# Stage one of three FFT batches: one float32 matmul a channel replaced by three float32r matmuls on split words

## The chip, the core and the metric

The kernel runs on one core of one Trainium2 chip. The metric is device time in microseconds (us), from the first to the last instruction plus what the device needs around them; lower is better. The engines that matter here are TensorE (PE, matmuls; PEld is its weight load), VectorE (DVE), ScalarE (ACT), GpSimd (POOL) and SyncE (SP, which here issues most DMAs). Each engine works through its own instructions in order; they meet at semaphores.

## The reference

The reference is a long convolution with a learned filter, followed by a two-layer MLP on every token:

```python
h_filt = (np.maximum(pos_emb @ w1, 0.0) @ w2) * np.exp(-0.01 * pos)[:, None]
u = x * v                                            # (4, 12480, 128)
Uf = np.fft.rfft(u, n=2 * S, axis=1)
Hf = np.fft.rfft(h_filt, n=2 * S, axis=0)
y = np.fft.irfft(Uf * Hf[None], n=2 * S, axis=1)[:, :S, :]
z = (x * y).reshape(49920, 128)
h = np.maximum(z @ w_in, 0.0)                        # 128 -> 2048
out = h * h @ w_out                                  # 2048 -> 128
```

There are four batches of 12,480 tokens with 128 channels. The convolution is done per batch, the MLP per token.

## The kernel before

The FFT is written as four matmul stages (`stage1` to `stage4`), with the time axis folded to 112 x 112 positions. `stage1` multiplies x by v, folds the two halves of each row (a sum and a difference, into a tile `ut` of 112 partitions x 4 channels x 120 columns), and multiplies each channel's 112 x 120 block with a table `ef` of 112 x 208. The filter and batch 0 run it in a first part of the program with `big=True`; that branch is not changed. Batches 1, 2 and 3 run `fft(b, done)`, in which `stage1(b, False)` is the first of four generators.

From about 320 us on, the program is one long loop over MLP chunks of 510 tokens. A *step* is one pass of its inner loop (L872 to L900): `m_h` makes six float32r matmuls into a PSUM tile `A` (two buffers), `m_o` makes six float32r matmuls for the step before last into `O`, ACT takes relu and square (`m_g`), DVE forms the product and the low word (`m_l`). Both operands of these matmuls are kept in two float32r words, high and low, and `mm3` (L97) adds the three products high-high, low-high and high-low. Between these the loop calls `adv(1)`, `adv(2)` and `adv(3)`, which move the FFT generator on to its next `yield`; a generator that stands at `yield 1` is moved by `adv(1)` alone. So the order on each engine is set by the code: at `adv(1)`, a stage 1 step issues the loads for three groups ahead, the products and folds (`mul`) for two groups ahead, and the eviction of the group before (`evac`); at `adv(3)` it issues `mm(t)`, the matmuls of one group of four channels. One step holds one group, and 32 groups make a batch. Before the first group, `mul(0)` and `mul(1)` are issued at the end of one step, and `mm(0)` comes at the end of the second step after that.

For these three batches `mul` runs on POOL (L278, L280, L281: product, sum, difference), `evac` on ACT (L316 to L318) and DVE (L309, L310). Pool `s1` has two buffers by default, three for `ut` (`halves`), three for `xt`, two for `vt`. A float32 matmul shows in the trace as two PE records; a float32r matmul as one. The rows name tiles by the program's names: `F` is one PSUM bank of stage results, `zi`, `zh` and `zl` are an MLP chunk's input and its two words (`zsplit`, once in eight steps), `gh` and `gl` the two words of the squared activations.

Of the kernel before, what the change touches and what calls it, by code (L numbers as in the profile page):

```python
# [7 lines left out]
F32 = mybir.dt.float32  # L8
F32R = mybir.dt.float32r
# [8 lines left out]
I = 112  # L18
C = 104
S = C * I  # L20
# [21 lines left out]
KP = 64 + HI  # L42
# [7 lines left out]
def hyena_moe_kernel(  # L50
# [19 lines left out]
    nc = tc.nc  # L70
# [14 lines left out]
    def pool(name, side="left", **kw):  # L85
        return tc.tile_pool(name=name, bufs=kw.pop("bufs", 2), side=side, reuse_waits="tile", **kw)

    def bank():
        return psf.tile([128, 512], F32, tag="F", name="F")
# [6 lines left out]

    def mm3(o, L, R, first=True, last=True):  # L97
        lh, ll = L
        rh, rl = R
        nc.tensor.matmul(o, lh, rh, start=first, stop=False)  # L100
        nc.tensor.matmul(o, ll, rh, start=False, stop=False)  # L101
        nc.tensor.matmul(o, lh, rl, start=False, stop=last)  # L102
# [48 lines left out]
    def first_rows():  # L151
        return W[:I].rearrange("p t (q d) -> p (t q) d", q=4)[:, : I + 1]
# [78 lines left out]
    def rest(k):  # L231
        for _ in range(k):
            yield 1
            yield 2
            yield 3

    def stage1(b, big, side="left", hook=None):
        DC = 4
        n = D // DC
        filt = b is None  # L240
        gap = HI + 1 if filt else HI
        with pool("s1", side) as p:
            ef = p.tile([I, 2, 2 * C] if big else [I, 2 * C], F32, name="ef", bufs=1)
            nc.sync.dma_start(out=ef, in_=e_tab[:, 2:4] if filt else e_tab[:, 0:2] if big else e_tab[:, 0])
            if not big:
                sign = p.tile([KP, 2], F32, name="sign", bufs=1)
                nc.gpsimd.memset(sign[:, 0:1], 1.0)
                nc.gpsimd.memset(sign[:, 1:2], -1.0)
            per = 2 if big else 1
            pa = 1  # L250
            L = {}
            halves = [p.tile([I, DC, KP], F32, name=f"ut{k}", bufs=1) for k in range(3)]
            for ut in halves:
                nc.gpsimd.memset(ut[:, :, gap:64], 0.0)

            def load(t):
                if filt or t >= n or t % per:
                    return
                xt = p.tile([128, per * DC, I], F32, tag="xt", name="xt", bufs=3)
                vt = p.tile([128, per * DC, I], F32, tag="vt", name="vt", bufs=3 if big else 2)  # L260
                queue = nc.gpsimd if big and t < early else nc.sync
                queue.dma_start(out=xt, in_=xs[b, :, t * DC : (t + per) * DC, :])
                queue.dma_start(out=vt, in_=vs[b, :, t * DC : (t + per) * DC, :])
                for k in range(per):
                    L[t + k] = [x[:I, k * DC : (k + 1) * DC] for x in (xt, vt)]

            def mul(t):
                if t >= n:
                    return
                ut = halves[t % 3]  # L270
                if filt:
                    f = first_rows()[:, :, t * DC : (t + 1) * DC].rearrange("p j d -> p d j")
                    eng = nc.vector
                    eng.tensor_add(out=ut[:, :, :gap], in0=f[:, :, HI:], in1=f[:, :, HI::-1])
                    eng.tensor_sub(out=ut[:, :, 64:], in0=f[:, :, HI + 1 :], in1=f[:, :, HI - 1 :: -1])
                else:
                    xt, vt = L[t]
                    (nc.vector if big else nc.gpsimd).tensor_mul(out=xt, in0=xt, in1=vt)  # L278
                    eng = nc.vector if big else nc.gpsimd
                    eng.tensor_add(out=ut[:, :, :HI], in0=xt[:, :, :HI], in1=xt[:, :, HI:])  # L280
                    eng.tensor_sub(out=ut[:, :, 64:], in0=xt[:, :, :HI], in1=xt[:, :, HI:])  # L281
                L[t] = ut

            def mm(t):
                u = L.pop(t)
                paired = big and t < n - 1
                if paired:
                    both = psa.tile([128, 2, 512], F32, tag="A", name="A")
                A = []
                for h in range(DC // 2):  # L290
                    A.append(both[:, h, :] if paired else bank())
                    for k in range(2):
                        o = A[h][:KP, k * 2 * C : (k + 1) * 2 * C]
                        if big:
                            nc.tensor.matmul(o[:64], u[:, 2 * h + k, :64], ef[:, 0, :], start=True, stop=True)
                            nc.tensor.matmul(o[64:], u[:, 2 * h + k, 64:], ef[:, 1, :], start=True, stop=True)  # L296
                        else:
                            nc.tensor.matmul(o, u[:, 2 * h + k, :], ef, start=True, stop=True)  # L298
                return A

            def evac(t, A):
                for h in range(DC // 2):
                    d0 = t * DC + 2 * h
                    view = W.rearrange("p t (k r d) -> p (t k) r d", k=2, r=2)[:, :C, :, d0 : d0 + 2]
                    src = A[h][:KP, : 4 * C].rearrange("p (d c r) -> p c r d", d=2, r=2)
                    if big:
                        (nc.vector.tensor_copy if h and t == n - 1 else nc.scalar.copy)(view, src)
                    elif h:
                        nc.vector.tensor_copy(view[:64], src[:64])  # L309
                        nc.vector.tensor_mul(  # L310
                            out=view[64:],
                            in0=src[64:, :, ::-1],
                            in1=sign[64:].rearrange("p (c r d) -> p c r d", c=1, d=1).to_broadcast([HI, C, 2, 2]),
                        )
                    else:
                        nc.scalar.copy(view[:64], src[:64])  # L316
                        nc.scalar.copy(view[64:, :, 0], src[64:, :, 1])
                        nc.scalar.mul(view[64:, :, 1], src[64:, :, 0], -1.0)  # L318

            la = 6 if big else 3  # L320
            early = 6 if big else 2
            for t in range(early):
                load(t)
                if big:
                    yield 1
            if not big:
                yield from rest(2)
            for t in range(pa + 1):
                mul(t)
            for t in range(early, la):  # L330
                load(t)
            yield 1
            yield 2
            prev = None
            for t in range(n):
                yield 1
                load(t + la)
                mul(t + pa + 1)
                if prev is not None:
                    evac(t - 1, prev)  # L340
                yield 2
                yield 3
                prev = mm(t)
                if hook is not None:
                    hook(t - n)
            yield 1
            evac(n - 1, prev)
# [332 lines left out]
    def fft(b, done):  # L680
        for name, gen in ("s1", stage1(b, False)), ("s2", stage2(False, False)), ("s3", stage3(False)), ("s4", stage4(b, done)):
            for k in gen:
                stage[0] = name
                yield k
# [41 lines left out]
    def during_s2(t):  # L726
# [3 lines left out]
        if t % TC == 0 and TH <= t // TC + 3 < NP // TC:  # L730
            table(t2s, t // TC + 3, tabs[0])

    s1f = stage1(None, True, "left")
    idle(10)
    filter_mlp(tables)
# [6 lines left out]
    raws = load_weights(wp)  # L742
    run(s1f)
    s1 = stage1(0, True, "right", during_s1)
    cvp = take("cvp")
    conv = [convert_weights(cvp, wp, raws, wt, range(k, 2 * NCW, 2)) for k in range(2)]
# [125 lines left out]
    for i in range(NM):  # L872
        for f in range(NS):
# [8 lines left out]
            while len(late) > len(tail):  # L882
                x, y, st = late.pop(0)
# [8 lines left out]
            n = i * NS + f  # L892
# [152 lines left out]
```

## Time and profile before

| | |
|---|---|
| median of 3 runs | 3071.08 us (3069.71 to 3072.46) |
| the profiled execution | 3062.8 us |
| its span, first to last instruction | 3060.9 us |
| PE busy | 3021.9 us, 99% of the span |
| DVE, ACT, POOL busy | 82%, 78%, 48% |
| stage 1 matmuls of batches 1 to 3 | 768 records, between 487.8 and 2009.1 us |

The page has the busy time of each engine, a picture of the span in 40 slices and the costliest groups. Matmul ends are modelled and overlap the next start, so the time that a stream of matmuls needs is read from start to start in the timeline, not from durations. The idle time in square brackets is what the engine waited before that instruction, and for whom.

### The profile page before, as it was taken

To read this page: it belongs to the slowest core of one execution; us is meant where nothing else is said; L and a number is where in the kernel's file an instruction comes from. 1 tells how busy PE (TensorE), PEld (TensorE's weight loads), DVE (VectorE), ACT (ScalarE), POOL (GpSimd) and SP (SyncE) were. 2 spreads that over 40 slices of the span, in tenths; PEclk is the share of its full clock that TensorE was granted. 3 is DMA by queue.
4 is the path that set the end of the run, shared out by engine and by line. 5 is a ranking of instruction groups with operands and counts; after the bars stand their busy time and mean duration, and the time that the engine had idled before them with its cause. 6 is when DMAs were issued, how large, how long until landed. Compare 5 with 4: busy or idle time off the path is not lost.

```text
span 3060.9 us, 48765 instructions
## 1 busy us (share of the span) xinstructions
PE 3021.9 (99%) x16010; PEld 2557.2 (84%) x16010; DVE 2510.9 (82%) x3056; ACT 2389.7 (78%) x3110; POOL 1469.1 (48%) x1595
## 2 busy tenths in 40 slices
PE   9989999999999999999999999999999999999999
PEld 8768888878888888888888888888888888888887
DVE  7888888878878988878877898878877898777776
ACT  5557777777888787788888877788888877888887
POOL 1249665647544665556544665646544563000000
PEclk9999999999999999999999999999999999999999
DMA  5782665444101664334200575434300474000000
GB/s 181 275 291 75 158 170 139 120 116 148 44 22 47 166 169 124 117 109 125 80 15 27 139 179 145 131 93 120 104 22 15 111 177 109 25 24 26 24 26 20
DMA packets 288753, 322.00 MB, mean 105 GB/s; under 512 B 95716, under 2 KB 214484, under 8 KB 288500
## 3 DMA queue, kind: packets, MB, share of 16 engines
q1 hardware_dynamic: 259348, 268.40, 30.3%
q0 software_dynamic: 29152, 50.48, 6.3%
q8 instruction: 128, 2.10, 0.3%
q14 instruction: 125, 1.02, 0.1%
HBM read 230.35 MB, written 64.55 MB: 96 GB/s over the span
## 4 chain that ended last, share of the span: by engine, by line
PE 88%; DMA 3%; DVE 3%; POOL 2%; issue 2%; ACT 1%; SPq 1%; DVEq 0%; ACTq 0%; POOLq 0%
PE A L100 11%; PE A L101 11%; PE A L102 11%; PE O L102 8%; PE O L101 8%; PE O L100 8%; PE F L386 5%; PE F L498 5%; PE F L298 4%; PE F L100 4%; PE F L102 4%; PE F L101 4%; PE A L296 2%; POOL W L411 1%; DMA xt<-x 1%
## 5 line engine op out<-in xcount | busy, mean ns | idle before, releaser
L800 ACT ACTIVATE r<-A 128x1020 f32<-128x1020 f32 (+2 forms) x784 | 804.2, 1026 | 410.7 <-PE A L102 397.1
L819 DVE TENSOR_TENSOR gl<-r,gh 128x1020 fp32r<-128x1020 f32 (+1 forms) x434 | 637.3, 1468 | 105.1 <-ACT r L807 68.1
L100 PE MATMUL A<-zh,wt 128*128 128x510 f32 (+2 forms) x1568 | 667.3, 426 | 1.8 <-DVE gl L819 1.5
L101 PE MATMUL A<-zh,wt 128*128 128x510 f32 (+2 forms) x1568 | 610.2, 389 | 0.0
L102 PE MATMUL A<-zl,wt 128*128 128x510 f32 (+2 forms) x1568 | 609.9, 389 | 0.0
L803 ACT ACTIVATE gh<-r 128x1020 fp32r<-128x1020 f32 (+1 forms) x452 | 477.3, 1056 | 61.0 <-PE O L101 53.3
L102 PE MATMUL O<-gl,wt 128*128 128x510 f32 (+1 forms) x1216 | 475.8, 391 | 3.6 <-DVE gl L819 3.5
L805 DVE SCALAR_TENSOR_TENSOR A<-A,r 128x1020 f32<-128x1020 f32 (+1 forms) x349 | 424.3, 1216 | 64.9 <-ACT r L800 63.0
L819 DVE TENSOR_TENSOR gl<-A,gh 128x1020 fp32r<-128x1020 f32 (+1 forms) x349 | 425.2, 1218 | 63.5 <-ACT gh L803 20.3
L101 PE MATMUL O<-gh,wt 128*128 128x510 f32 (+1 forms) x1216 | 472.1, 388 | 0.0
L100 PE MATMUL O<-gh,wt 128*128 128x510 f32 (+1 forms) x1216 | 472.0, 388 | 0.0
L807 ACT ACTIVATE r<-r 128x1020 f32<-128x1020 f32 (+1 forms) x435 | 461.0, 1060 | 12.5
L814 DVE CAST gh<-r 128x1020 fp32r<-128x1020 f32 (+1 forms) x332 | 232.6, 701 | 211.7 <-ACT r L807 210.7
L783 POOL TENSOR_TENSOR zl<-zi,zh 128x510 fp32r<-128x510 f32 (+1 forms) x97 | 126.6, 1305 | 536.1 <-PE A L102 427.7
L571 POOL TENSOR_TENSOR al<-W,ah 104x512 fp32r<-104x512 f32 x214 | 282.2, 1319 | 187.8 <-ACT ah L565 185.8
L102 PEld LDWEIGHTS A<-zl,wt 128*128 128x128 f32 x1568 | 294.4, 188 | 63.1
L507 POOL TENSOR_TENSOR W<-c 104x224 f32<-104x224 f32 x256 | 215.5, 854 | 264.6 <-ACT c L505 261.5
L100 PEld LDWEIGHTS A<-zh,wt 128*128 128x128 f32 x1568 | 296.0, 189 | 51.2 <-DVE gl L819 4.7
L101 PEld LDWEIGHTS A<-zh,wt 128*128 128x128 f32 x1568 | 296.3, 189 | 42.7
L423 POOL TENSOR_TENSOR W<-W,m 112x256 f32<-112x256 f32 x156 | 167.9, 1076 | 229.0 <-DVE m L421 207.0
L102 PEld LDWEIGHTS O<-gl,wt 128*128 128x128 f32 x1216 | 228.0, 187 | 53.0 <-DVE gl L819 5.7
L101 PEld LDWEIGHTS O<-gh,wt 128*128 128x128 f32 x1216 | 227.8, 187 | 47.5
(126 smaller groups left out, 5413.2 us busy)
## 6 DMA issues: line engine op xcount, KB each, us to landing
ht<-Hd SPq DMA_DIRECT2D x208, 256.0 KB
tb<-t POOLq DMA_DIRECT2D x224, 208.0 KB, 3.5
xt<-x SPq DMA_DIRECT2D x224, 128.0 KB
xt<-xs SPq DMA_DIRECT2D x96, 224.0 KB
vt<-vs SPq DMA_DIRECT2D x96, 224.0 KB
zd<-zs SPq DMA_DIRECT2D x333, 64.0 KB
out<-ot SPq DMA_DIRECT2D x79, 255.0 KB
tb<-t2s SPq DMA_DIRECT2D x156, 112.0 KB
```

The lines of the kernel that those rows point to most:

```text
L100: nc.tensor.matmul(o, lh, rh, start=first, stop=False)
L101: nc.tensor.matmul(o, ll, rh, start=False, stop=False)
L102: nc.tensor.matmul(o, lh, rl, start=False, stop=last)
L423: nc.gpsimd.tensor_sub(out=re[0], in0=re[0], in1=im[1])
L507: nc.gpsimd.tensor_sub(out=dst[:, 1], in0=c[:, :, 0:3:2], in1=c[:, :, 3:0:-2])
L571: eng.tensor_sub(out=lo, in0=w, in1=hi.bitcast(F32))
L800: nc.scalar.activation(r, h, AF.Relu)
L803: nc.scalar.activation(hi, r, AF.Square)
L805: nc.vector.scalar_tensor_tensor(out=h, in0=h, scalar=0.0, in1=r, op0=ALU.max, op1=ALU.mult)
L807: nc.scalar.activation(r, r, AF.Square)
L814: nc.vector.tensor_copy(hi, g)
L819: nc.vector.tensor_sub(out=lo, in0=g, in1=hi.bitcast(F32))
```

## The change

For the three batches the table `ef` and each group's folds `ut` are split into two float32r words, and each channel's one float32 matmul becomes the three float32r matmuls of `mm3`. The high word of `ut` is copied by ACT in even groups and by DVE in odd ones (480 values in each of 112 partitions); the low word is a subtraction on POOL. The split of a group is issued one step ahead of its matmuls, behind the `mul` for two groups ahead; `split(0)` is issued in the setup, behind `mul(1)`.

```diff
             if not big:
+                eh, el = (p.tile([I, 2 * C], F32R, name=f"e{k}", bufs=1) for k in range(2))
                 sign = p.tile([KP, 2], F32, name="sign", bufs=1)
...
-            L = {}
+            L, S = {}, {}
...
+            def split(t):
+                if big or t >= n:
+                    return
+                u = L[t]
+                hi, lo = (p.tile([I, DC, KP], F32R, tag=k, name=k) for k in ("uh", "ul"))
+                (nc.vector.tensor_copy if t % 2 else nc.scalar.copy)(hi, u)
+                nc.gpsimd.tensor_sub(out=lo, in0=u, in1=hi.bitcast(F32))
+                S[t] = hi, lo
+
             def mm(t):
                 u = L.pop(t)
+                words = S.pop(t, None)
...
-                            nc.tensor.matmul(o, u[:, 2 * h + k, :], ef, start=True, stop=True)
+                            mm3(o, [x[:, 2 * h + k, :] for x in words], (eh, el))
...
+            if not big:
+                nc.scalar.copy(eh, ef)
+                nc.vector.tensor_sub(out=el, in0=ef, in1=eh.bitcast(F32))
+            split(0)
             yield 1
             yield 2
...
                 load(t + la)
                 mul(t + pa + 1)
+                split(t + 1)
                 if prev is not None:
                     evac(t - 1, prev)
```

The change adds 16 lines, so L278 of before is L279 after, L281 is L282, L316 is L327, L800 is L816, L803 is L819.

POOL at the start of batch 1's stage 1 before: three instructions a group (product, sum, difference), in the order of the groups.

```order
L278 TENSOR_TENSOR xt_5345<-xt_5345,vt_5346 112x448
L280 TENSOR_TENSOR ut0_5339<-xt_5345 112x4x56
L281 TENSOR_TENSOR ut0_5339<-xt_5345 112x4x56
L278 TENSOR_TENSOR xt_5349<-xt_5349,vt_5350 112x448
L280 TENSOR_TENSOR ut1_5340<-xt_5349 112x4x56
L281 TENSOR_TENSOR ut1_5340<-xt_5349 112x4x56
L278 TENSOR_TENSOR xt_5403<-xt_5403,vt_5404 112x448
L280 TENSOR_TENSOR ut2_5341<-xt_5403 112x4x56
L281 TENSOR_TENSOR ut2_5341<-xt_5403 112x4x56
```

The same place on POOL after; `ul` is the low word that the group's matmuls read.

```order
L279 TENSOR_TENSOR xt_5347<-xt_5347,vt_5348 112x448
L281 TENSOR_TENSOR ut0_5341<-xt_5347 112x4x56
L282 TENSOR_TENSOR ut0_5341<-xt_5347 112x4x56
L279 TENSOR_TENSOR xt_5351<-xt_5351,vt_5352 112x448
L281 TENSOR_TENSOR ut1_5342<-xt_5351 112x4x56
L282 TENSOR_TENSOR ut1_5342<-xt_5351 112x4x56
L291 TENSOR_TENSOR ul_5412<-ut0_5341,uh_5411 112x480
L279 TENSOR_TENSOR xt_5405<-xt_5405,vt_5406 112x448
L281 TENSOR_TENSOR ut2_5343<-xt_5405 112x4x56
L282 TENSOR_TENSOR ut2_5343<-xt_5405 112x4x56
L291 TENSOR_TENSOR ul_5443<-ut1_5342,uh_5442 112x480
```

Each group has a fourth instruction, and the low word of group 0 stands behind all of group 1's folds: before, group 0's matmuls were released by POOL's third instruction, now by its seventh.

ACT at the same place before: relu (L800) and square (L803) of four steps, then the eviction of group 0.

```order
L800 ACTIVATE r_5390<-A_5377 128x2x510
L803 ACTIVATE gh_5391<-r_5390 128x2x510
L800 ACTIVATE r_5420<-A_5407 128x2x510
L803 ACTIVATE gh_5421<-r_5420 128x2x510
L800 ACTIVATE r_5447<-A_5434 128x2x510
L803 ACTIVATE gh_5448<-r_5447 128x2x510
L316 COPY W_71<-F_5454 64x208x2
```

The same place on ACT after.

```order
L816 ACTIVATE r_5392<-A_5379 128x2x510
L819 ACTIVATE gh_5393<-r_5392 128x2x510
L344 CAST e0_5336<-ef_5334 112x208
L290 CAST uh_5411<-ut0_5341 112x480
L816 ACTIVATE r_5428<-A_5415 128x2x510
L819 ACTIVATE gh_5429<-r_5428 128x2x510
L816 ACTIVATE r_5459<-A_5446 128x2x510
L819 ACTIVATE gh_5460<-r_5459 128x2x510
L290 CAST uh_5487<-ut2_5343 112x480
L327 COPY W_71<-F_5466 64x208x2
```

The table's high word and group 0's high word stand ahead of the next two steps' relu and square, and group 2's high word ahead of the eviction of group 0.

## Rows read from the trace of the kernel before

**Rows 1.** The page, parts 1 and 2: busy time; granted TensorE clock by slice.

```profile
PE 3021.9 (99%) x16010; PEld 2557.2 (84%) x16010; DVE 2510.9 (82%) x3056; ACT 2389.7 (78%) x3110; POOL 1469.1 (48%) x1595
...
PEclk9999999999999999999999999999999999999999
```

**Rows 2.** Timeline, PE, one step: start us, us, engine, line, op, tiles, shape, count.

```profile
521.02 1.57 PE L298 MATMUL F<-ef,ut 112*120 112x208 f32 x8
...
522.67 0.39 PE L101 MATMUL A<-zh,wt 128*128 128x510 f32 x1
...
524.94 0.39 PE L102 MATMUL O<-gl,wt 128*128 128x510 f32 x1
525.17 1.57 PE L298 MATMUL F<-ef,ut 112*120 112x208 f32 x8
```

**Rows 3.** Line 298's instructions: records, ns min/median/max, first and last start.

```profile
L298 PE MATMUL F<-ef,ut x768: 336/339/437, 487.8 to 2009.1; 112*120 112x208 f32 x192
```

**Rows 4.** Timeline, PE, stage 4 of batch 0: first float32r matmul of 256 columns, and sixth.

```profile
1007.85 0.28 PE L100 MATMUL F<-ah,tb 104*128 104x256 f32 x1
...
1008.44 0.28 PE L102 MATMUL F<-al,tb 104*128 104x256 f32 x1
```

**Rows 5.** Timeline, DVE, the step of rows 2.

```profile
525.06 1.23 DVE L805 SCALAR_TENSOR_TENSOR A<-A,r 128x1020 f32<-128x1020 f32 x1 [0.46 <-ACT r L800]
526.42 1.22 DVE L819 TENSOR_TENSOR gl<-A,gh 128x1020 fp32r<-128x1020 f32 x1
527.56 0.57 DVE L309 COPY W<-F 64x416 f32<-64x416 f32 x1
528.15 0.59 DVE L310 TENSOR_TENSOR W<-F,sign 56x416 f32<-56x416 f32 x1
```

**Rows 6.** Timeline, POOL and ACT, the same step.

```profile
522.74 0.67 POOL L280 TENSOR_TENSOR ut<-xt 112x224 f32<-112x224 f32 x1 [1.73 <-PE F L298]
...
524.00 1.03 ACT L800 ACTIVATE r<-A 128x1020 f32<-128x1020 f32 x1 [0.90 <-PE A L102]
```

**Rows 7.** Groups by form, DVE and ACT: shapes, count, busy us, mean ns, idle before.

```profile
L814 DVE CAST gh<-r 128x1024 fp32r<-128x1024 f32 x144 | 99.7, 693 | 86.7 <-ACT r L807 86.7
...
L782 ACT CAST zh<-zi 128x510 fp32r<-128x510 f32 x79 | 47.7, 604 | 0.8 <-DMA zi<-zd 0.8
```

**Rows 8.** Timeline, POOL and DVE, at 1506 us.

```profile
1505.85 0.85 POOL L424 TENSOR_TENSOR W<-W,m 112x256 f32<-112x256 f32 x1
...
1506.29 0.96 DVE L814 CAST gh<-r 128x1020 fp32r<-128x1020 f32 x1 [1.12 <-ACT r L807]
```

**Rows 9.** Timeline, POOL, start of stage 1 in batches 1, 2 and 3.

```profile
485.16 1.16 POOL L278 TENSOR_TENSOR xt<-xt,vt 112x448 f32<-112x448 f32 x1 [2.66 <-DMA vt<-vs]
...
487.67 1.15 POOL L278 TENSOR_TENSOR xt<-xt,vt 112x448 f32<-112x448 f32 x1
...
490.14 1.16 POOL L278 TENSOR_TENSOR xt<-xt,vt 112x448 f32<-112x448 f32 x1
...
1170.66 1.17 POOL L278 TENSOR_TENSOR xt<-xt,vt 112x448 f32<-112x448 f32 x1 [9.88 <-DMA vt<-vs]
...
1175.60 1.29 POOL L783 TENSOR_TENSOR zl<-zi,zh 128x510 fp32r<-128x510 f32 x1
...
1876.21 1.16 POOL L278 TENSOR_TENSOR xt<-xt,vt 112x448 f32<-112x448 f32 x1 [7.85 <-DMA vt<-vs]
```

**Rows 10.** Timeline, PE, the first stage 1 matmuls of batches 1, 2 and 3.

```profile
487.76 0.44 PE L298 MATMUL F<-ef,ut 112*120 112x208 f32 x1
...
1173.24 0.96 PE L298 MATMUL F<-ef,ut 112*120 112x208 f32 x4 [1.35 <-POOL ut L281]
...
1879.29 1.57 PE L298 MATMUL F<-ef,ut 112*120 112x208 f32 x8
```

**Rows 11.** Windows: stretch, length, engines' busy us (count), PEclk, DMA share, GB/s.

```profile
115.00:118.00 3.00, 0.12 (x1) 0.12 (x2) 2.72 (x7) 0.76 (x2) 1.98 (x4) 1.00 1.03 419
118.00:121.50 3.50, 3.50 (x10) 2.58 (x11) 3.33 (x13) 1.68 (x4) 0.79 (x2) 0.56 1.01 395
```

## The prediction

> **What bounds the kernel now.** I read the page first, then the timeline of PE in stage 1, then the other engines in the same step, then the three places where stage 1 begins. The page shows PE busy for 99% of the span at a full granted clock [rows 1], so time that PE is spared is time won, and time that PE waits is time lost, one for one.
>
> In stage 1 a step repeats every 4.15 us, from one group's first matmul at 521.02 to the next at 525.17 [rows 2]. Ten MLP matmuls lie between the starts at 522.67 and 524.94, 0.227 us each; twelve are 2.72 us. What is left, 1.42 us, is the group of four float32 matmuls, eight records of 0.178 us. There are 768 records [rows 3], so 96 groups, 32 a batch.
>
> The others have slack, of different size. DVE's four instructions run from 525.06 to 528.74, so 3.68 us of 4.15, and its wait is 0.46 us for ACT [rows 5]. ACT waits 0.90 us for PE; POOL waits 1.73 us for a `ut` buffer that the matmuls still read [rows 6].
>
> At the start of a batch POOL waits for the first `vt` load, then runs its folds with no pause, and PE has already caught up with it: in batch 2 it waits 1.35 us for them, in batch 3 its first matmul comes 0.6 us after the first folds are done [rows 9, 10].
>
> **PE's group of matmuls.** Eight records go, twelve float32r matmuls of 208 columns come. No row has float32r with under 256 columns. Six of 256 columns start from 1007.85 to 1008.44, 0.118 us apart [rows 4]; with 0.227 us for 510, a straight line through the two gives 0.098 us for 208. So one pass costs between 0.098 and 0.118 us, 1.18 to 1.42 us a group. Each matmul also has its own weight load, 120 columns against 128 in the 256-column row, and that does not shrink with the moving columns, so I take 0.105: 1.26 us, a saving of 0.16 us, and a PE step of 3.98 us. Beyond these ends, if float32r at this width needed the passes of float32, each would cost a float32 matmul's 0.355 us, 4.26 us a group; that is a rival below.
>
> The Trainium skill ("TensorE: Matmul & The Clock Gate", section "LDWEIGHTS (loading the stationary operand)") puts a load at its columns over 1.2 GHz, an estimate of 100 ns for 120 columns. By that rule a group would be 1.20 us and the PE step 3.92 us. No row here shows loads alone as the limit.
>
> **The split words in the steady step.** POOL gains a subtraction of 480 values. Its neighbour of 510 values takes 1.29 us, and 1.2 us is the share for 480. The three instructions of a group come 2.51 and 2.47 us apart [rows 9], so POOL goes to 3.7 us; one `zl` in eight steps adds 0.16: 3.85 us. It fits only because the wait for `ut` goes: that buffer is now read by the split alone, a step earlier.
>
> ACT gains, every second step, a cast; 604 ns for 510 values [rows 7] makes 0.57 us, mean 0.28, inside its 0.90 us of slack. It costs nothing while the step stays above 3.6 us.
>
> DVE gains the cast in the other steps. 693 ns for 1024 values [rows 7] gives 0.33 us by size, and with a fixed part I take 0.40: DVE's mean goes from 3.68 to 3.88 us. But POOL is now nearly always at work, and the trace shows what that does to a DVE cast between SBUF tiles: the one that starts at 1506.29, while POOL's subtraction runs from 1505.85 to 1506.70, takes 0.96 instead of 0.69 us [rows 7, 8]: it waited 0.27 us, until POOL was nearly through. The wait w for POOL in front of a cast lies between 0 (POOL idle) and 1.2 us (the longest POOL instruction of a group just begun). The mean over instructions of 1.16, 0.67, 0.67 and 1.2 us met at a random point is about 0.5; as the cast beside it waited 0.27, I take 0.35. DVE's mean step is then 3.68 + (0.40 + 0.35) / 2 = 4.06 us. In return POOL is kept out for the 0.40 us of every second step, which brings it to 4.05 us.
>
> The Trainium skill ("SBUF — State Buffer", section "SBUF: two separate sides") says that the port pair shared by DVE and GpSimd is an exclusive lock, held for a whole instruction. The row agrees. By that rule with the full 0.5 us, DVE's step would be 4.13 us, 2 us would be won in 96 steps, and the time would be 3084 us.
>
> So the steady step is set by DVE and POOL, not PE: 4.07 us, 0.08 us under today's. Over 96 steps that is 7.5 us won. The ends are 3.92 us (22 us won) and 4.2 us (5 us lost).
>
> **The starts of the batches.** PE's first group now needs the low word of group 0, which stands behind group 1's folds on POOL.
> - Batch 1: POOL is through both folds at 490.14 [rows 9], the low word is done at 491.35, and the matmuls that began at 487.76 [rows 10] begin 3.6 us later.
> - Batch 2: both folds end at 1175.60, the low word at 1176.8 against 1173.24: 3.6 us. Then POOL has `zl`, group 2's folds and group 1's low word, 1.25 + 2.47 + 1.2 us, until 1181.7, where PE arrives at 1176.8 + 1.26 + 2.72 = 1180.8: 0.9 us more.
> - Batch 3: 1876.21 + 4.95 + 1.2 = 1882.4 against 1879.29: 3.1 us, and 0.6 us where `zl` comes between.
>
> Together 11.8 us. Nothing gives it back, since PE is the bound afterwards. I see no earlier start for the folds: they wait for DMAs, which the change does not move on SP's queue. Behind these waits stand others. Group 0's high word holds ACT from about 482.5 until the folds are done at 487.7, and the relu of the next step, today at 483.8, is queued behind it; it ends at 489.3, DVE's two instructions at 491.7, and PE wants that `A` buffer at 492.6, after the late group. So this delay is covered by the first one, with 0.9 us to spare. Splitting the table (an ACT and a DVE instruction of 208 values, 0.3 us each) lies in the two steps, 5.4 us, between the setup and the first group.
>
> A last price of these gaps is the clock. After the gap at 115 us, where PE worked 0.12 us of 3.00, the granted clock was 0.56 over the next 3.50 us [rows 11], so mostly the 1.2 GHz level; 0.44 x 3.5 = 1.5 us lost. Three gaps of 3.1 to 4.9 us could cost 0 to 4.6 us; I take two of them, 3 us.
>
> **The sum.** -7.5 + 11.8 + 3 = +7.3 us. The profiled execution took 3062.8 us (span 3060.9 and 1.9 around it), so it would take 3070; the median of the runs lies 8.3 us above that execution, and the same difference on 3071.1 gives 3078 us.
>
> **Rivals.**
> - *Faster: the steady saving is whole.* Matmuls at 0.098 us (a PE step of 3.90 us) and casts that meet POOL between instructions (DVE at 3.88 us) allow a step of 3.92 us: 22 us won, 11.8 lost, clock untouched, 3061 us. For it speaks the straight line of two float32r rows; against it, that DVE and POOL both must fit into 3.92 us with nothing to spare. It decides from a step of 3.96 us down.
> - *The two cancel.* A step of 4.00 us wins 14 us, the starts take 12 to 15: 3071 us.
> - *DVE becomes the bound above today's step.* With w of 0.6 us, 3.68 + 0.5 = 4.18: 3 to 5 us lost on top of 15, 3090 us. For it: POOL's load of over 90%, and DVE's present slack of only 0.46 us; against it, the small wait in [rows 8].
> - *The change does not do what it says on PE.* If float32r at 208 columns takes the passes of float32, the group grows by 2.84 us, 272 us in all, and with the starts the time is about 3355 us. For it: every float32r row has 256 columns or more. Against it: the rows of 256 and 510 lie on one line, with no sign of a step.
>
> **How the numbers follow.** Forecast 0.45 (3070 to 3086), faster 0.16, cancel 0.14, DVE-bound 0.13, float32's passes 0.12. A difference of 0.2%, 6 us, is about what can be told from none here: 3065 to 3077. Faster holds the first rival, 0.16; no change holds the cancelling case and 0.18 of the forecast, 0.32; slower holds the rest, 0.52. The range leaves out the float32-pass case and half of the fastest: 3061 to 3098 us.
>
> **What would show it.** In the timeline of PE: twelve records of 208 columns a group, 0.105 us apart (0.35 refutes the step on PE); steps of 4.0 to 4.1 us, with short waits for `gl`, `A` or `ul`; gaps of 3 to 5 us before the first group of each batch that end at POOL's low word, with a granted clock under 1.00 behind some. In the rows of DVE, casts from `ut` to `uh` that take 0.4 to 1.6 us. The forecast is wrong if the gaps are under 2 us or the steady step is under 3.96 us.

## The result and the profile after

| | before | after |
|---|---|---|
| median | 3071.19 us (3069.71 to 3072.46, 4 runs) | 3098.51 us (3096.93 to 3099.75, 4 runs) |
| ratio, 95% interval | 1 | 1.0097 [1.0085, 1.0109] |
| profiled execution, span | 3062.8, 3060.9 us | 3097.3, 3095.5 us |
| first matmul of group 0 to that of group 1, batches 1, 2, 3 | 4.24, 4.24, 4.15 us | 8.57, 9.02, 8.58 us |
| mean of the 30 steps behind it | 4.147 in each | 4.321, 4.310, 4.222 us |

The change made the kernel 27.3 us slower by these medians, 1.0089 of before; the recorded ratio is a little higher, and before's medians in the later rounds are 2 to 3.5 us lower than here. The forecast was 3078, with a range up to 3098: the measured time lies 0.5 us above that end. The direction was right, the size was not. The last two lines of the table are taken from the starts of the groups' first matmuls.

Parts 1 and 2 of the page after, the lines that answer to [rows 1]: PE has more busy time, but a smaller share of the span.

```profile
PE 3026.9 (98%) x16394; PEld 2550.4 (82%) x16394; DVE 2551.9 (82%) x3107; ACT 2419.2 (78%) x3161; POOL 1588.3 (51%) x1691
...
PEclk9999999999999999999999999999999999999999
```

The timeline of PE in a step that waits for nothing (columns as in [rows 2]).

```profile
506.27 0.26 PE L100 MATMUL F<-e,uh 112*120 112x208 f32 x1
506.36 0.27 PE L101 MATMUL F<-e,ul 112*120 112x208 f32 x1
506.47 0.27 PE L102 MATMUL F<-e,uh 112*120 112x208 f32 x1
...
507.52 0.41 PE L100 MATMUL A<-zh,wt 128*128 128x510 f32 x1
...
510.26 0.26 PE L100 MATMUL F<-e,uh 112*120 112x208 f32 x1
```

Twelve records take 1.25 us, 0.105 each, and the step is 3.99 us against 4.15. So PE got the saving that was forecast; the loss lies in other steps. In batch 1, behind four of 4.00, they go 4.78, 4.00, 5.54, 4.00, 4.64, 4.01, 4.11, 4.00 and so on, in a pattern that comes back every eight steps, one MLP chunk.

What happens once a chunk stands in the timeline of SP's DMA queue and in that of POOL.

```profile
536.30 0.33 SPq L264 DMA_DIRECT2D vt<-vs  x1
542.02 0.34 SPq L855 DMA_DIRECT2D out<-ot  x1
542.42 2.76 SPq L790 DMA_DIRECT2D zi<-zd  x5
545.28 0.65 SPq L263 DMA_DIRECT2D xt<-xs  x1
546.02 0.38 SPq L264 DMA_DIRECT2D vt<-vs  x1
```

```profile
545.10 1.23 POOL L291 TENSOR_TENSOR ul<-ut,uh 112x480 fp32r<-112x480 f32 x1
550.35 1.15 POOL L279 TENSOR_TENSOR xt<-xt,vt 112x448 f32<-112x448 f32 x1 [4.02 <-DMA vt<-vs]
551.58 0.67 POOL L281 TENSOR_TENSOR ut<-xt 112x224 f32<-112x224 f32 x1
552.20 0.67 POOL L282 TENSOR_TENSOR ut<-xt 112x224 f32<-112x224 f32 x1
552.83 1.22 POOL L291 TENSOR_TENSOR ul<-ut,uh 112x480 fp32r<-112x480 f32 x1
554.00 1.15 POOL L279 TENSOR_TENSOR xt<-xt,vt 112x448 f32<-112x448 f32 x1
```

SP's queue works in order. From 536.30 to 542.02 it issues nothing, as the next in it is the store of a chunk's output; then five `zi` loads take 2.76 us, and only then come the `xt` and `vt` loads. POOL waits 4.02 us. The timeline of POOL before has the same pause, which the prediction left out:

```profile
537.88 1.14 POOL L278 TENSOR_TENSOR xt<-xt,vt 112x448 f32<-112x448 f32 x1 [5.54 <-PE O L102]
```

The profile names PE there; in two other chunks of batch 1 it names the load, 5.04 us at 505.1 and 5.68 us at 604.4. SP's queue before has the same five `zi` loads ahead of the `vt` load:

```profile
530.53 2.77 SPq L774 DMA_DIRECT2D zi<-zd  x5
...
533.91 0.40 SPq L263 DMA_DIRECT2D vt<-vs  x1
```

Before, POOL waited 1.73 us for a `ut` buffer in an ordinary step [rows 6]; the pause took the place of some of these waits and cost nothing. After, a group costs POOL 3.65 us, from 550.35 to 554.00: 8 x 3.65 + 1.25 for `zl` + 4.0 = 34.5 us in eight steps, 4.31 a step. From the end of this pause to the end of the next the trace has 35.0 us (550.35 to 585.33), with no other wait of POOL over 0.1 us; the mean of batches 1 and 2 comes out at 4.31 to 4.32 because the first steps behind the start wait for little. In batch 3, at 4.22, the pauses are shorter, 2.4 to 3.3 us. POOL never wins its lead back at 4.00 us a step, because the next pause comes first.

How this reaches PE: rows of PE in the step of 5.54 us, and of ACT and DVE ahead of it.

```profile
527.03 0.26 PE L100 MATMUL F<-e,uh 112*120 112x208 f32 x1
527.82 0.36 PE L101 MATMUL F<-e,ul 112*120 112x208 f32 x1 [0.52 <-POOL ul L291]
...
528.32 0.27 PE L102 MATMUL F<-e,uh 112*120 112x208 f32 x1
529.14 0.33 PE L100 MATMUL F<-e,uh 112*120 112x208 f32 x1 [0.55 <-DVE W L321]
...
532.58 0.26 PE L100 MATMUL F<-e,uh 112*120 112x208 f32 x1
```

```profile
517.86 0.60 ACT L290 CAST uh<-ut 112x480 fp32r<-112x480 f32 x1 [2.53 <-POOL ut L282]
...
519.48 1.02 ACT L816 ACTIVATE r<-A 128x1020 f32<-128x1020 f32 x1
```

```profile
520.54 1.23 DVE L821 SCALAR_TENSOR_TENSOR A<-A,r 128x1020 f32<-128x1020 f32 x1 [2.24 <-ACT r L816]
...
523.04 1.14 DVE L290 CAST uh<-ut 112x480 fp32r<-112x480 f32 x1
...
528.40 0.59 DVE L321 TENSOR_TENSOR W<-F,sign 56x416 f32<-56x416 f32 x1
```

PE waits twice in one group: for the low word, which stands on POOL behind the folds that were late, and for a PSUM bank `F` that DVE has not yet emptied. DVE is late since two steps before it ACT's cast had waited 2.53 us for POOL's folds, with eviction and relu queued behind it; DVE waited 2.24 us for that relu, took 1.14 us for its own cast and then worked without a pause until the bank was free at 528.99.

The instructions on tile `uh` by kind: count, then ns min/median/max.

```profile
L291 POOL TENSOR_TENSOR ul<-ut,uh x96: 1201/1227/1243, 495.4 to 2037.9; 112x480 fp32r<-112x480 f32 x96
L290 ACT CAST uh<-ut x48: 582/594/599, 493.1 to 2031.4; 112x480 fp32r<-112x480 f32 x48
L290 DVE CAST uh<-ut x48: 398/995/1416, 497.1 to 2037.4; 112x480 fp32r<-112x480 f32 x48
```

The same cast takes 0.59 us on ACT every time, and on DVE 0.40 alone, 1.00 in the median and 0.88 in the mean: a wait w of 0.60 or 0.48 beside a POOL that works nearly all the time. What it waits for can be read off. In 39 of the 48 casts on DVE a POOL instruction was running at the start, and each of them ended 0.26 to 0.27 us after that instruction, whichever line it was; the other nine took 0.40. For the cast shown above, from 523.04 to 524.18, it is this one, which ends at 523.92:

```profile
522.62 1.30 POOL L799 TENSOR_TENSOR zl<-zi,zh 128x510 fp32r<-128x510 f32 x1
```

The starts of batches 1, 2 and 3 on PE, which answer to [rows 10], and the granted clock behind the first (columns as in [rows 11]).

```profile
493.70 0.36 PE L100 MATMUL F<-e,uh 112*120 112x208 f32 x1 [0.70 <-ACT uh L290]
496.68 0.36 PE L101 MATMUL F<-e,ul 112*120 112x208 f32 x1 [2.62 <-POOL ul L291]
...
498.27 0.63 PE L101 MATMUL A<-zh,wt 128*128 128x510 f32 x1
498.69 0.63 PE L102 MATMUL A<-zl,wt 128*128 128x510 f32 x1
...
1190.47 0.36 PE L100 MATMUL F<-e,uh 112*120 112x208 f32 x1 [1.94 <-ACT uh L290]
1193.46 0.53 PE L101 MATMUL F<-e,ul 112*120 112x208 f32 x1 [2.63 <-POOL ul L291]
...
1907.25 0.36 PE L100 MATMUL F<-e,uh 112*120 112x208 f32 x1
1910.23 0.36 PE L101 MATMUL F<-e,ul 112*120 112x208 f32 x1 [2.63 <-POOL ul L291]
```

```profile
497.90:501.30 3.40, 3.40 (x11) 2.65 (x11) 3.25 (x5) 2.07 (x5) 3.40 (x4) 0.52 0.51 134
```

PE starts group 0 with its high word and stands still for the low one. Behind that, in batch 1, the clock is at 0.52, mostly the 1.2 GHz level, and a matmul of 510 columns takes 0.42 us instead of 0.227.

**The balance.** The 90 steps behind the starts: 30 x (4.321 + 4.310 + 4.222 - 3 x 4.147) = +12.4 us. The three first steps: 26.17 - 12.63 = +13.5 us, low word and clock together. The waits ahead of group 0: 0.70 + 1.94 - 1.35 [rows 10] = +1.3 us. Sum 27.2, the measured 27.3; that they agree to 0.1 us is luck. The sum is that of two profiled executions, whose spans lie 34.6 us apart; of the other 7.4 us, 2.2 lie ahead of the first MLP step, in code that is the same, and the rest between the stretches summed here.

### The profile page after: what moved, and what is told of

Same layout as the page of the kernel before. It is cut to its first block, busy times and chain, and to the rows that moved or that the text cites. A ratio compares the mean times of both kernels' runs of the same rounds, so it can differ in the third digit from the quotient of the medians.

```text
span 3095.5 us, 49682 instructions
## 1 busy us (share of the span) xinstructions
PE 3026.9 (98%) x16394; PEld 2550.4 (82%) x16394; DVE 2551.9 (82%) x3107; ACT 2419.2 (78%) x3161; POOL 1588.3 (51%) x1691
## 4 chain that ended last, share of the span: by engine, by line
PE 78%; POOL 7%; DVE 5%; DMA 4%; issue 2%; ACT 2%; SPq 1%; DVEq 0%; POOLq 0%; ACTq 0%
PE A L100 10%; PE A L101 10%; PE A L102 10%; PE O L102 7%; PE O L100 7%; PE O L101 7%; PE F L402 5%; PE F L514 5%; PE F L100 5%; PE F L101 5%; PE F L102 5%; DMA vt<-vs 2%; POOL xt L279 2%; PE A L307 2%; POOL ul L291 1%
## 5 line engine op out<-in xcount | busy, mean ns | idle before, releaser
L816 ACT ACTIVATE r<-A 128x1020 f32<-128x1020 f32 (+2 forms) x784 | 804.1, 1026 | 362.9 <-PE A L102 347.2
L819 ACT ACTIVATE gh<-r 128x1020 fp32r<-128x1020 f32 (+1 forms) x452 | 477.7, 1057 | 55.3 <-PE O L101 46.2
```

What stands on the lines that cost most here:

```text
L816: nc.scalar.activation(r, h, AF.Relu)
L819: nc.scalar.activation(hi, r, AF.Square)
```

## The experiments

Twelve of the thirteen kernels are the changed kernel with a further edit; `e11_before_deep` is the kernel before with one. Before's median over the runs beside them lay between 3067.7 and 3069.1 us. A gain over the changed kernel is given against its 3098.51, which was measured beside a before of 3071.19, so 2 to 3 us of it can be the round.

| run | median us | ratio to before | first steps, batches 1, 2, 3 | mean of the 30 later steps |
|---|---|---|---|---|
| e1_act_hi | 3094.77 | 1.0081 [1.0066, 1.0096] | 8.63, 9.63, 8.21 | 4.29, 4.26, 4.25 |
| e2_deep_loads | 3077.68 | 1.0029 [1.0018, 1.0041] | 8.58, 9.54, 6.59 | 4.08, 4.08, 4.15 |
| e3_start | 3097.72 | 1.0095 [1.0080, 1.0110] | 7.97, 7.03, 6.24 | 4.34, 4.45, 4.33 |
| e4_no_low | 3093.83 | 1.0078 [1.0063, 1.0093] | 6.38, 8.81, 7.49 | 4.32, 4.29, 4.23 |
| e5_swap | 3134.34 | 1.0211 [1.0196, 1.0226] | 9.83, 9.28, 8.31 | 4.64, 4.68, 4.66 |
| e6_swap_rest | 3123.03 | 1.0174 [1.0157, 1.0191] | 4.00, 3.99, 4.00 | 4.71, 4.68, 4.71 |
| e7_act_deep | 3071.28 | 1.0010 [1.0001, 1.0019] | 8.58, 9.55, 8.60 | 4.00, 4.00, 4.00 |
| e8_all | 3096.58 | 1.0093 [1.0078, 1.0108] | 4.00, 3.99, 4.00 | 4.46, 4.43, 4.45 |
| e9_act_deep_rest | 3058.09 | 0.9961 [0.9947, 0.9974] | 4.01, 4.00, 4.00 | 4.00, 4.00, 4.00 |
| e10_rest | 3089.09 | 1.0065 [1.0051, 1.0078] | 4.00, 4.39, 3.99 | 4.39, 4.25, 4.40 |
| e11_before_deep | 3069.12 | 1.0005 [0.9995, 1.0016] | 4.24, 4.24, 4.15 | 4.15, 4.15, 4.15 |
| e12_f32_mm | 3071.26 | 1.0011 [1.0002, 1.0020] | 4.14, 4.14, 4.13 | 4.15, 4.14, 4.14 |
| e13_late_split | 3049.51 | 0.9938 [0.9925, 0.9952] | 3.99, 4.00, 3.99 | 4.00, 4.00, 4.00 |

**e1_act_hi.** All high words on ACT.

```diff
-                (nc.vector.tensor_copy if t % 2 else nc.scalar.copy)(hi, u)
+                nc.scalar.copy(hi, u)
```

> The changed kernel with every group's high word copied by ACT; DVE has no cast left. Theory A (late loads: POOL, nearly full, stands some 4 us once a chunk behind loads that SP issues late, and sets a mean step of 4.3 us): POOL's work and its loads stay as they are, so the time stays within 4 us of the changed kernel's 3098.5. Theory B (DVE's casts wait for POOL, 1.0 us in the median, DVE comes late to the PSUM banks, and PE's waits for them, 12.5 us in the three stages, are the loss): about 12 us less, 3086. ACT's added 0.6 us in odd steps costs nothing in either (0.9 us of slack).

Only 3.7 us were won, and the interval overlaps that of the changed kernel (1.0085 to 1.0109). DVE's cast is not what bounds the steady step while POOL is late.

**e2_deep_loads.** More buffers for the loads, and these issued two groups earlier.

```diff
-                xt = p.tile([128, per * DC, I], F32, tag="xt", name="xt", bufs=3)
-                vt = p.tile([128, per * DC, I], F32, tag="vt", name="vt", bufs=3 if big else 2)
+                xt = p.tile([128, per * DC, I], F32, tag="xt", name="xt", bufs=3 if big else 5)
+                vt = p.tile([128, per * DC, I], F32, tag="vt", name="vt", bufs=3 if big else 4)
...
-            la = 6 if big else 3
+            la = 6 if big else 5
```

> The changed kernel with xt in five and vt in four buffers and loads five groups ahead instead of three, so that a hold-up on SP's queue of 6 us does not reach POOL. Theory A (late loads): POOL's pause once a chunk goes, PE's waits for the low word in the steady steps go with it, 10 us less, 3088. Theory B (DVE's casts): within 3 us of 3098.5, since the casts meet POOL as often as before.

20.8 us were won, more than expected: the late load was the main cause of the long steps. The row of PE's waits for the low word (us, times, longest) shows it, first after, then this run.

```profile
PE F L101 <- POOL ul L291: 13.6, 16, 2.6
```

```profile
PE F L101 <- POOL ul L291: 7.6, 3, 2.6
```

The three left are those of the starts. PE's waits for DVE's bank go from 9.1 us (21 times) to 3.2 (11). The steps are now 4.08 us in batches 1 and 2, against the 4.07 of the forecast, and DVE is the bound as forecast: its cast has a mean of 0.79 us here, a w of 0.39 near the 0.35 taken, 3.68 + 0.79 / 2 = 4.07, and between 568 and 606 us the profile lists one wait of it, 0.34 us. In batch 3 they are 4.15: the first step is 2.0 us shorter than in the changed kernel, and the next ones give that back.

**e3_start.** The table's split and group 0's ahead of group 1's folds.

```diff
+                if t == 0 and not big:
+                    nc.scalar.copy(eh, ef)
+                    nc.vector.tensor_sub(out=el, in0=ef, in1=eh.bitcast(F32))
+                    split(0)
...
-            split(0)
             yield 1
```

> The changed kernel with the split of the table and of group 0 issued ahead of group 1's product and folds, so that group 0's low word is POOL's fourth instruction and not its seventh. Theory C (the starts cost PE 9 us of idle time and the clock that falls after them 6.5 us): idle time at each start falls to about 1.2 us and the granted clock stays whole: 12 us less, 3086.5. Rival to C: POOL has no time in hand, so group 1 now waits for what group 0 won, and later groups too: within 4 us of 3098.5, with the clock still whole.

Nothing was won. The first steps shrink by 0.6 to 2.3 us, but the later ones grow to 4.33 to 4.45: with POOL as the bound, time given back at the start is taken again. Both theories had the clock whole, and it was not: 0.50 was granted from 497.80 to 501.10 and from 1194.10 to 1197.40 us.

**e4_no_low.** No subtraction on POOL.

```diff
-                hi, lo = (p.tile([I, DC, KP], F32R, tag=k, name=k) for k in ("uh", "ul"))
+                hi = p.tile([I, DC, KP], F32R, tag="uh", name="uh")
...
-                nc.gpsimd.tensor_sub(out=lo, in0=u, in1=hi.bitcast(F32))
-                S[t] = hi, lo
+                S[t] = hi, hi
```

> The changed kernel without the low word of the folds: the high word stands in its place in the matmuls, and POOL has its three instructions a group as before (the output is that of the rounded folds). Theory A: POOL falls to 2.5 us a step, no pause reaches PE, steps go to PE's 4.00 us and the starts lose under 1 us each: 96 x 0.147 = 14 us below before's 3071, 3058. Theory B: the casts still meet POOL's instructions (POOL busy 60%), steps of 4.1 us: about 3068.

Neither came: 4.7 us were won, with an interval that overlaps the changed kernel's. POOL had a third less to do, ran ahead, and then waited for the same load; ACT's cast passed the wait on, and PE waited 16.2 us in all for banks that DVE emptied late. The two rows, of POOL and of ACT:

```profile
543.94 1.16 POOL L279 TENSOR_TENSOR xt<-xt,vt 112x448 f32<-112x448 f32 x1 [10.99 <-DMA vt<-vs]
```

```profile
546.50 0.59 ACT L290 CAST uh<-ut 112x480 fp32r<-112x480 f32 x1 [2.23 <-POOL ut L282]
```

So it is the lateness of the load that costs, not POOL's amount of work alone: with the work gone the steps stay at 4.23 to 4.32.

**e5_swap, e6_swap_rest.** The split of group t+1 ahead of the folds of t+2 (swap); and then, in addition, two more steps between setup and group 0 (rest).

```diff
                 yield 1
+                split(t + 1)
                 load(t + la)
                 mul(t + pa + 1)
-                split(t + 1)
```

```diff
             if not big:
-                yield from rest(2)
+                yield from rest(3)
...
             split(0)
+            if not big:
+                yield from rest(1)
             yield 1
```

> The changed kernel with one edit in the loop: the split of the next group stands ahead of the load and the folds two groups ahead, not behind them; buffers and loads as in the changed kernel. Theory A2 (it is the place in the queue: a low word whose inputs are ready stands on POOL behind folds that wait for a late load): PE's steady waits for low words go as they did with deeper loads, 3078. Rival A1 (POOL's total pace, work plus pause, is the bound wherever the low word stands): the steps keep their mean of 4.3 us, within 5 us of 3098.5. The starts are as before in both: the low word of group 0 still stands behind group 1's folds.

> The swap, and two more MLP steps at the start of each batch: one between the first loads and the first folds, one between the split of group 0 and its matmuls. Theory C2 (the starts cost 16 us because POOL and ACT wait for loads and folds with PE's next work queued behind them; time between them, which MLP steps fill, removes the whole of it): no gap before a first group, the granted clock whole from 310 us on, 15 us less than the swap alone, 3063 if that is at 3078. Rival: the start's loss only moves into later groups, as it did when group 0's split alone came earlier: within 4 us of the swap.

The swap cost 35.8 us, against both theories. A row of POOL in e5_swap shows why:

```profile
531.32 1.24 POOL L291 TENSOR_TENSOR ul<-ut,uh 112x480 fp32r<-112x480 f32 x1 [1.29 <-DVE uh L290]
```

In the changed kernel the folds of group t+2 cover the cast of group t+1. With the swap POOL's low word stands right behind the folds that the cast reads, and POOL waits for ACT or DVE in 89 of the 96 groups, 0.3 to 1.4 us each. The rest did what it was to do: first steps of 4.00 us, no clock lost at the starts, 11.3 us won over the swap alone.

**e7_act_deep, e8_all.** e1 and e2 together; and then with swap and rest as well.

> Deeper loads (five xt, four vt, five groups ahead) and every high word on ACT. Theory B2 (with the load pause gone, what is left of the steady loss, steps of 4.08 instead of PE's 4.00, is DVE coming late to the PSUM banks after casts that met POOL): steps go to 4.00, some 7 us less than the deeper loads alone, 3071. Rival (ACT, 3.8 us a step with the cast, becomes late in its place): within 3 us of 3078.

> All four edits: high words on ACT, deeper loads, split ahead of the folds, and the two MLP steps at the start. By A2, B2 and C2 together nothing but PE is left: steps of 4.00 us, no gaps, the whole saving of 96 x 0.147 = 14 us under before, 0.995 to 0.996 of it, 3055 to 3057. Rival (the split work costs somewhere else what PE wins): no faster than before, 3069.

e7_act_deep is 6.4 us faster than e2 and runs at 4.00 us, and PE's waits for DVE's bank in stage 1 are gone; only the starts stand between it and a gain. e8_all loses it all again to the swap: POOL's folds of 2.5, a wait of 0.70 and a low word of 1.2 make the 4.4 us between these rows.

```profile
528.45 1.24 POOL L291 TENSOR_TENSOR ul<-ut,uh 112x480 fp32r<-112x480 f32 x1 [0.71 <-ACT uh L290]
...
532.87 1.23 POOL L291 TENSOR_TENSOR ul<-ut,uh 112x480 fp32r<-112x480 f32 x1 [0.70 <-ACT uh L290]
```

**e9_act_deep_rest, e10_rest, e11_before_deep, e12_f32_mm.** e7 with the rest; the rest alone; the kernel before with e2's edit; e9 with `nc.tensor.matmul(o, u[:, 2 * h + k, :], ef, start=True, stop=True)` in place of `mm3`.

> After with the high words all on ACT, the deeper loads, and two more steps between setup and group 0 (one of them behind group 0's split), the order in the loop unchanged. Theory A (three separable causes: late loads, DVE's cast, late low word at the starts): steps of 4.00 us as in the run with ACT and deep loads, first step 4.0 to 4.2 in each batch, no gap over 1 us at the starts, clock whole. Won against before: 96 x (4.147 - 4.00) = 14 us, so 3054 to 3058 us against 3069. Rival B (the gaps at the starts only come back elsewhere, as in the experiment that moved the table's split): some other wait of 3 us a batch and steps above 4.05; 3066 to 3072 us.

> After with only the two more steps between setup and group 0. Theory A: first steps 4.0 to 4.2 instead of 8.6 to 9.0, the clock whole behind them, about 9 + 6.5 us won; steady steps as in after, 4.2 to 4.3; 3080 to 3086 us. Rival B (POOL, being the bound in the steady step, owes those folds anyway and a later start only shifts where PE waits): under 5 us won, 3094 to 3098 us.

> Before, with the deeper buffers and earlier loads of the run with deep loads, nothing else. Theory A (the late loads cost nothing while POOL had 1.7 us of slack a step): steps of 4.15 us, 3067 to 3071 us, no difference. Rival B (the deep loads are a gain of their own): 3058 to 3064 us.

> After with the high words all on ACT, the deeper loads and the two more steps, all splits issued, but each channel's matmul is the one float32 matmul of before on the unsplit operands; the words are written and not read. Tells the price of the split from the gain of the matmuls. Theory A (once the waits are gone, PE alone sets the step): steps of 4.15 us, 3067 to 3072 us, as before. Rival B (the split still costs): steps above 4.2, 3075 us or more.

e9_act_deep_rest is 10.3 us faster than before, 3058.09 at the edge of what theory A allowed. But its claim of no gap over 1 us failed: PE waits ahead of each batch for the MLP's product, as this row of PE ahead of batch 2 shows (1.49 us in batch 1, 2.50 in batch 3). The window around it has the full clock.

```profile
1182.24 0.50 PE L100 MATMUL A<-zh,wt 128*128 128x510 f32 x1 [2.64 <-DVE gl L837]
```

```profile
1181.00:1185.00 4.00, 2.76 (x12) 2.33 (x13) 3.51 (x4) 3.13 (x4) 3.92 (x5) 1.00 0.46 139
```

e10_rest came out between the two theories: 9.4 us won. The first steps gave 13.8 us, but the later steps, still bound by POOL, took 5.5 us back (30 x 13.035 against 30 x 12.853). e11_before_deep shows no difference: before, the late loads were free. In e12_f32_mm all the split's work runs beside steps of 4.14 us and nothing waits for it there; the time is 2.8 us above before, with waits of the kind just shown at the starts, and 13.2 above e9, about what the float32r matmuls alone are worth (96 x 0.15 = 14.4).

**e13_late_split.** e9 with the table's split and group 0's one step later, behind the relu of the next step.

```diff
             if not big:
+                yield from rest(1)
                 nc.scalar.copy(eh, ef)
                 nc.vector.tensor_sub(out=el, in0=ef, in1=eh.bitcast(F32))
             split(0)
-            if not big:
-                yield from rest(1)
             yield 1
```

> The kernel with the high words on ACT, deeper loads and two more steps, but with the table's split and group 0's split issued one step later, behind the next step's relu and square instead of ahead of them. Theory A (group 0's high word on ACT, which waits for POOL's folds, holds the relu queued behind it, and PE then waits for the product's A buffer: 1.49, 2.64 and 2.50 us ahead of the three batches): these three waits go, no gap over 1 us within 12 us ahead of a batch's first group, steps 4.00, 6 us less than the run without it: 3050 to 3054 us against 3068 to 3069. Rival B (the relu is late because of something else around the start, such as the input's cast or the loads): the waits for the product stay or move, 3056 to 3059 us.

Theory A, 0.5 us under its range: 3049.51 us, 8.6 less than e9 (five runs each, and one of e9's, 3049.64, lies among e13's), and the trace shows no wait of PE in the 12 us ahead of any of the three batches. First the two ACT rows of e9, then those of e13: the cast that waited 1.58 us for the folds with the relu behind it now waits for nothing.

```profile
493.61 0.60 ACT L290 CAST uh<-ut 112x480 fp32r<-112x480 f32 x1 [1.58 <-POOL ut L282]
494.11 1.02 ACT L818 ACTIVATE r<-A 128x1020 f32<-128x1020 f32 x1
```

```profile
497.28 0.59 ACT L290 CAST uh<-ut 112x480 fp32r<-112x480 f32 x1
497.78 1.02 ACT L817 ACTIVATE r<-A 128x1020 f32<-128x1020 f32 x1
```

This is the fastest version, 18.2 us under before (ratio 0.9938 [0.9925, 0.9952]): 14.4 us are the 96 shorter steps, 1.35 the wait that before has in batch 2; the other 2.4 us are within the interval.

## Why the prediction was wrong

- **PE's group: right.** 0.105 us a matmul, as taken, though that was a choice between two bounds; no sign of float32's passes. The prediction's reason against these, that the rows of 256 and 510 columns lie on one line, says nothing, as any two do. An undisturbed step is 4.00 us (forecast 3.98).
- **The steady step: wrong, and this is the step that failed.** "... so POOL goes to 3.7 us; one `zl` in eight steps adds 0.16: 3.85 us. It fits only because the wait for `ut` goes ..." The work was right (3.65 us a group), but the sum of POOL had no term for waiting on its loads, a wait of 2.4 to 4.2 us once a chunk. The trace of before had that wait, once a chunk, hidden in the slack that the change used up. -7.5 us was forecast, +12.4 came. e2, which takes the late load away, gives back 20.8 us and lands on the forecast's own step in two of the three batches; e11 shows that the same edit is worth nothing before.
- **The casts on DVE: somewhat undersized.** w was taken as a mean of 0.35; the measured mean is 0.48 in after and 0.39 where the loads are early. Taking DVE's casts away is worth 3.7 us beside late loads (e1) and 6.4 without them (e2 to e7). The rival with w = 0.6 came nearest in time (3090), but DVE was not the bound: without its casts e1 is at 3094.77.
- **ACT's cast "costs nothing": half right.** In e13 ACT has twice as many and the step is 4.00. But where POOL is late, the cast holds eviction and relu behind it, which is how e4 lost what it saved.
- **The starts: right in kind, close in size.** Forecast 3.6, 4.5 and 3.7 us, 11.8 in all. Measured, from the first idle to the second matmul less a matmul's 0.105: 3.6, 4.8 less the 1.35 of before, and 2.9 us, so 9.9 us.
- **The delayed relu "covered by the first one, with 0.9 us to spare": right, and it hid a loss.** Once the first wait was gone, 1.49 + 2.64 + 2.50 us came to light (e9), and e13 took them away.
- **The clock: undersized.** 3 us taken, 5.5 measured (the three first steps less 4.00 and less the wait for the low word). The lower level came at all three gaps, not at two, and stayed for longer in batch 2, where it began inside the gap, behind PE's wait of 1.94 us ahead of the group.

The later steps of e10 are slower than after's in batches 1 and 3 and faster in batch 2. POOL's waits for `vt` behind the starts go the same way: 3.8 to 4.5 us in batch 1 (after: 3.8 to 4.0), 3.4 to 4.7 in batch 3 (after: 2.4 to 3.3), and in batch 2 one of 4.5, then 2.5 to 3.1 (after: 3.7 to 4.2). So the load's lateness is at work there too. Not settled: why the same load comes later in one batch than in another.

## What to carry to other kernels

Before giving work to an engine that has slack, look for the waits that the slack hides: list every long wait of that engine over a whole period (here a chunk of eight steps, not one step) and add them to its work. When one queue carries loads and a store that waits for late results, the loads must be issued early enough to outlast the store's wait. A cast that feeds another engine's instruction belongs where that engine has other work to do meanwhile, and not ahead of something that the main engine waits for: e8 and e9 differ by 38.5 us in the place of one line.

## What the runs showed of the hardware

- A float32r matmul of 208 columns starts every 0.105 us, between the 0.097 of a straight line through 256 and 510 columns and the 0.118 of 256 columns [rows 4].
- One cast of 112 x 480 values in after: 0.58 to 0.60 us on ACT. On DVE 0.40 us where POOL stood still at its start, and otherwise what was left of POOL's instruction and 0.26 to 0.27 us more, up to 1.42 us.
- The gaps inside group 0 of after, 2.6 us of idle PE each, came with a lower clock, 0.52 granted over 3.4 us behind the first. The gap of 2.64 us in e9 did not: 1.00 in the window around it. Another in e9, of 2.36 us at 401.55, did: 0.50 granted from 403.10 to 406.40 us. So the length of a gap alone does not tell whether the clock falls.
